# Decay scans of four head pairs in one instruction, GpSimd's products on VectorE, and another issue order in a gated-attention and feed-forward kernel

## The chip, the cores and the metric

The program runs on one core of one Trainium2 chip. The metric is the device time of one execution in microseconds. Three runs of the kernel before took 741.72, 742.07 and 739.28 us; their median is 741.72 us.

## The reference

A gated linear attention over 2 batches, 8 heads, 768 steps and a head dimension of 48 is followed by a gated feed-forward layer and by four weighted experts. All inputs are float32.

```python
def _attn_ref(q, k, v, alpha):
    state = np.zeros((B, H, D, D), dtype=np.float32)
    for t in range(S):
        state = alpha[:, :, t, :, None] * state + np.einsum('bhd,bhe->bhde', k[:, :, t], v[:, :, t])
        y[:, :, t] = np.einsum('bhd,bhde->bhe', q[:, :, t], state)

def _moe_ref(x, w_gate, w_val, w_out, rms_g):        # 1536 tokens, 384 -> 1536 -> 384
    rms = np.sqrt(np.mean(x * x, axis=-1, keepdims=True) + 1e-06)
    xn = x / rms * rms_g
    g = xn @ w_gate
    return (g * (1.0 / (1.0 + np.exp(-g))) * (xn @ w_val)) @ w_out

def _moe2_ref(x, domain_probs, w1, w2):              # 4 experts, 384 -> 1024 -> 384
    p = domain_probs / (domain_probs.sum(-1, keepdims=True) + 1e-09)
    for e in range(E):
        out += p[:, e:e + 1] * (np.maximum(x @ w1[e], 0.0) @ w2[e])
```

The output of the attention, with the heads side by side, is the input of the first layer, and its output is the input of the experts.

## The kernel before

The 768 steps are cut into six chunks of 128, each for two batches: 12 pairs of a chunk and a batch. For a pair, `a_prep` makes decays within the chunk: for each of four head pairs `j` one scan that runs backwards over the steps with a floor (L578, tile `fut`), a reciprocal of its last value (L586), one scan that runs from there to 1 (L592, in the tile `akq`), and then products with k (`KENG`) and q (`QENG`) in halves of two head pairs (L553 on GpSimd, L555 on VectorE). The tables `KENG`, `QENG`, `SENG`, `MENG`, `TENG`, `LENG` and `WENG` name the engine of such a piece for each chunk or weight unit. `a_score` makes the products of k and q (L648) and masks them: for chunks 0 to 3 a copy on ScalarE (L668) and a select on GpSimd (L673), for the others one product on VectorE (L663). `a_y` makes the chunk's output (L687), `a_state` turns k (L718), copies it (L722), makes the state's part of the chunk (L732) and adds it to the state (L755), and the state is decayed at the next chunk's `a_prep` (L631, L636). `a_rms` norms by token (L766 to L794; the power on GpSimd is L779), turns the features onto the partitions (L801), and writes them as a high and a low part (L812, L818, or L830, L838, L843).

The layers work on blocks of 512 tokens: chunks 0 and 1 are block 0, chunks 2 and 3 block 1, chunks 4 and 5 block 2. Every dense product is made in three passes of high and low parts (`mm3`, L856 to L858). The weights of the first layer come as the bits of doubles, in 18 half units; `w_conv` turns each into float bits in three VectorE instructions (L493, L501, L509) and into a high part (ScalarE, L470) and a low part (L476, on VectorE or GpSimd as `WENG` says). For each of 12 tiles `f` of the first layer there are two products (`up1`: gate, value; tile `g`), an activation (L901), a product with the value (L909, tile `s`), its high part (L913) and low part (L920, tile `hl`), and a closing product (`outs`, tile `o`), one step behind. Block 0 goes through its tiles in pieces of 256 columns, half by half:

```python
    steps = [(0, h, 6 * g + f) for g in range(2) for h in (h0, h1) for f in range(6)]
```

`block1` then handles block 1, and after the attention's pools are closed block 2, each with 512 columns, and the experts follow with 96 steps of an up product (tiles `g`, `ph`) and four closing products (tiles `o`, `pe`).

The order of the instructions is set by `Plan`: every operation names its engine, a rough cost, and what it reads and writes; `schedule` then issues, engine by engine, what can start first, by the longest path to the end plus a number for its group (`BIAS`), with two numbers (`MARGIN`, `SLIP`) for how long an engine may be held for something more urgent. On the chip each engine then works through its own queue in that order. While TensorE has to wait for the first chunk, `idle` puts products of zeros (L1001) in its queue, as many as the plan's wait holds. After the layers, a check on the decays (`fit`) decides whether `general`, a slower way for decays that a chunk can't carry, is run.

Of the kernel before, what the change touches and what calls it, by code (L numbers as in the profile page):

```python
# [36 lines left out]
KENG = ["POOL", "POOL", "DVE", "POOL", "POOL", "POOL"]  # L37
QENG = ["DVE", "POOL", "DVE", "POOL", "POOL", "POOL"]
SENG = ["POOL", "POOL", "DVE", "DVE", "POOL", "POOL"]
MENG = ["ACT", "ACT", "ACT", "ACT", "DVE", "DVE"]  # L40
TENG = ["POOL", "POOL", "DVE", "POOL", "DVE", "DVE"]
LENG = ["DVE", "POOL", "DVE", "POOL", "DVE", "DVE"]
HENG = ["DVE", "DVE", "DVE"]
WENG = ["POOL", "DVE", "POOL", "DVE", "POOL", "POOL", "POOL", "DVE", "DVE", "DVE", "POOL", "POOL", "POOL", "DVE", "DVE", "POOL", "DVE", "POOL"]
BIAS = {"c00": 407.1, "c01": 773.8, "w0": -431.2, "": -1780.3, "w5": -1413.1, "c3": -559.1, "w1": -383.5, "s0": -331.4, "c4": -1817.3, "w2": -1907.8, "w4": -996.0, "c1": 501.5, "c5": 48.1, "c2": -2420.3, "guard": -1215.8, "w3": -630.2}
MARGIN, SLIP = 18.01, 3.18


class Tile:
    """A tile that is allocated when its first writer is issued."""  # L50
# [12 lines left out]
class Plan:  # L63
    """Instructions in the order of their meaning, issued in the order of a list schedule.

    Each operation names its engine, a rough cost, and the (parts of) tiles it reads and writes.
    The schedule goes by the longest path to the end; it changes when things are issued, and
    nothing about what is computed."""
# [22 lines left out]
    def op(self, eng, cost, fn, r=(), w=(), chain=None, after=()):  # L91
# [23 lines left out]
        self.ops.append([eng, cost, fn, deps, self.group, before])  # L115
        return i

    def schedule(self):
# [14 lines left out]
        # tiles: who waits for a slot (for the path only)  # L133
# [46 lines left out]
        for _ in range(n):  # L180
# [15 lines left out]
            busy[e] = end  # L196
            for x in uses.get(pick, ()):
# [15 lines left out]
    def issue(self, idle=None, until=None):  # L213
        """idle(us) is called for each wait of the tensor engine up to operation until."""
# [10 lines left out]
def general(tc, const, akq, kf, vf, w64, w32, out):  # L225
    """Everything once more for decays that the products of a chunk can't carry: the state by
    one scan over the sequence for each of its columns, the layers in float32."""
# [4 lines left out]
    with ExitStack() as ctx:  # L232
        dram = ctx.enter_context(tc.tile_pool(name="xs_p", bufs=1, space=bass.MemoryType.DRAM))
        xs = dram.tile([B, DM, S], F32, name="xs")
        with ExitStack() as att:
# [6 lines left out]
            for b in range(B):  # L242
                for j in range(NP):
                    a, k, q = (sb.tile([HP, NC, C], F32, name=f"in{i}") for i in range(3))
                    for t, src in ((a, akq[:, b, :, 0, j]), (k, kf[:, b, :, j]), (q, akq[:, b, :, 2, j])):
                        nc.sync.dma_start(out=t, in_=src.rearrange("c p s -> p c s"))
# [3 lines left out]
                        out=vt, in_=vf[:, b, :, 2 * j * D : 2 * (j + 1) * D].rearrange("c s e -> s c e")  # L250
# [157 lines left out]
def body(ctx: ExitStack, tc: tile.TileContext, ar, akq, v, kf, vf, w64, w32, rms_g, probs, out):  # L408
# [18 lines left out]
    floor = const.tile([P, C + 1], F32, name="floor")  # L427
# [38 lines left out]
    def hilo(key, src, src_ap, lo_eng):  # L466
# [6 lines left out]
        eng, cost = ("POOL", 1.77) if lo_eng is nc.gpsimd else ("DVE", 0.87)  # L473
        plan.op(
            eng, cost,
            lambda: lo_eng.tensor_tensor(  # L476
# [6 lines left out]
    def w_conv(u):  # L483
        """Bits of doubles to bits of floats, then hi + lo."""
# [33 lines left out]
    akq_t, v_t, f_t, at_t, S_t, x1_t = {}, {}, {}, {}, {}, {}  # L518
    guard_n = [0]

    def a_load(c, b, chain=None):
        if c == 1:
            t = plan.tile(x1p, [P, 3, NP, C], F32, ("x1h", "x1l")[b], 2)
            f = plan.tile(wpool, [P, HW], F32, "wlo", 18)
        else:
            t = plan.tile(att, [HP, 3, NP, C], F32, "akq", 2)
            f = plan.tile(att, [HP, NP * (C + 1)], F32, "fut", 2)
        fut = lambda: f()[:HP, : NP * (C + 1)].rearrange("p (j s) -> p j s", j=NP)
        dma(
            0.23, lambda: nc.sync.dma_start(out=fut(), in_=ar[c, b]), w=[(f, 0), (f, 1)],  # L530
            chain=chain,
        )
        for i in range(3):
            dma(
                0.23, lambda i=i: nc.sync.dma_start(out=t()[:HP, i], in_=akq[c, b, :, i]),
                w=[(t, i, 0), (t, i, 1)], chain=chain,
            )
        akq_t[c, b], f_t[c, b] = t, (f, fut)
# [11 lines left out]
    def mul(kind, out, a, b, r, w):  # L550
# [758 lines left out]
```

## Time and profile before

| | us |
|---|---|
| median of three runs | 741.72 |
| lowest and highest run | 739.28, 742.07 |
| span of the profiled execution | 737.2 |
| TensorE busy in the span | 702.5 |
| VectorE busy | 323.0 |
| ScalarE busy | 205.0 |
| GpSimd busy | 99.8 |

The span runs from the first to the last of the program's own instructions; the median of the runs is 4.5 us above it, for what lies around the span. A TensorE instruction's time contains its way through the array, so that neighbours overlap: the pace of products is read from one start to the next. VectorE's records overlap by some 0.07 us in the same way.

### The profile page before, as it was taken

Reading aid. Unit: us, or ns where it says so; the run is one execution under the profiler, and the core shown is the slowest. Engines: PE = TensorE matmul, PEld = TensorE weight load, DVE = VectorE, ACT = ScalarE, POOL = GpSimd, SP = SyncE. Lnnn points to the kernel's source line nnn. Section 1 sums busy time; section 2 is a strip of 40 time slices with the busy share of each in tenths; the row PEclk is TensorE's granted clock in tenths of the full one; section 3 lists DMA queues with packets and bytes.
Section 4 is the critical chain, followed back from the end, with each engine's and each line's share of the span. In section 5 each row is a group of like instructions: output and inputs, shape, how many; then the busy total and the mean of one; then the engine's idle time right before and its main releaser. Section 6 shows DMA issues by size and latency. Waiting matters only on the chain.

```text
span 737.2 us, 10392 instructions
## 1 busy us (share of the span) xinstructions
PE 702.5 (95%) x4330; PEld 623.7 (85%) x4330; DVE 323.0 (44%) x565; ACT 205.0 (28%) x434; POOL 99.8 (14%) x127
## 2 busy tenths in 40 slices
PE   7678897999999999999999999999999999999996
PEld 5577896898888888879989999899998999989995
DVE  8989999757322344452313341214412121312212
ACT  4544354444322243441112321112211111111110
POOL 5957224644000000000000000000000000000000
PEclk9988999999999999999999999999999999999999
DMA  9944472235000023221000220001000000001001
GB/s 270 264 139 168 139 222 74 74 96 190 4 0 1 2 85 129 86 85 44 1 0 1 86 86 0 1 1 44 0 1 1 0 1 1 1 0 44 12 32 48
DMA packets 15416, 44.85 MB, mean 61 GB/s; under 512 B 2048, under 2 KB 5120, under 8 KB 15360
## 3 DMA queue, kind: packets, MB, share of 16 engines
q1 hardware_dynamic: 15072, 44.07, 18.7%
q8 instruction: 36, 0.59, 0.3%
q14 instruction: 20, 0.16, 0.1%
q10 hardware_dynamic: 288, 0.03, 0.0%
HBM read 40.94 MB, written 3.15 MB: 60 GB/s over the span
## 4 chain that ended last, share of the span: by engine, by line
PE 80%; DVE 14%; issue 3%; DMA 1%; ACT 1%; POOL 0%; SPq 0%; DVEq 0%; POOLq 0%; ACTq 0%
PE g L856 10%; PE g L857 10%; PE g L858 10%; PE o L856 9%; PE o L858 9%; PE o L857 9%; PE ph L857 5%; PE ph L858 5%; PE ph L856 4%; PE pe L857 2%; PE pe L856 2%; PE pe L858 2%; DVE akq L592 2%; DVE cv L493 2%; DVE cv L501 2%
## 5 line engine op out<-in xcount | busy, mean ns | idle before, releaser
L856 PE MATMUL g<-x1l,whi 128*128 128x512 f32 (+1 forms) x432 | 156.6, 362 | 6.7 <-DVE s L909 6.2
L858 PE MATMUL g<-x1h,wlo 128*128 128x512 f32 (+1 forms) x432 | 154.7, 358 | 2.7 <-DVE wlo L476 2.6
L857 PE MATMUL g<-x1h,whi 128*128 128x512 f32 (+1 forms) x432 | 154.4, 357 | 0.0
L856 PEld LDWEIGHTS g<-x1l,whi 128*128 128x128 f32 x432 | 82.3, 190 | 18.6 <-DVE s L909 7.0
L858 PE MATMUL o<-whi,hl 128*128 128x384 f32 x288 | 97.5, 338 | 0.0
L856 PE MATMUL o<-wlo,hh 128*128 128x384 f32 x288 | 97.2, 338 | 0.0
L857 PE MATMUL o<-whi,hh 128*128 128x384 f32 x288 | 96.9, 336 | 0.0
L858 PEld LDWEIGHTS g<-x1h,wlo 128*128 128x128 f32 x432 | 82.3, 191 | 14.5 <-DVE wlo L476 3.1
L857 PEld LDWEIGHTS g<-x1h,whi 128*128 128x128 f32 x432 | 82.4, 191 | 10.1
L1173 DVE SCALAR_TENSOR_TENSOR hl<-ph,hh 128x512 fp32r<-128x512 f32 x48 | 33.2, 691 | 128.2 <-ACT hh L1168 128.2
L1173 DVE SCALAR_TENSOR_TENSOR hl<-g,hh 128x512 fp32r<-128x512 f32 x48 | 33.1, 689 | 119.0 <-ACT hh L1168 119.0
L1168 ACT ACTIVATE hh<-g 128x512 fp32r<-128x512 f32 x48 | 28.7, 597 | 162.9 <-PE g L858 162.9
L1168 ACT ACTIVATE hh<-ph 128x512 fp32r<-128x512 f32 x48 | 28.7, 597 | 155.0 <-PE ph L858 153.8
L909 DVE TENSOR_TENSOR s<-g,s 128x256 f32<-128x256 f32 (+1 forms) x48 | 26.6, 554 | 78.3 <-PE g L858 74.1
L856 PEld LDWEIGHTS o<-wlo,hh 128*128 128x128 f32 x288 | 54.1, 188 | 4.2
L857 PEld LDWEIGHTS o<-whi,hh 128*128 128x128 f32 x288 | 54.0, 188 | 4.1
L858 PE MATMUL ph<-x1h,wlo 128*128 128x512 f32 x144 | 57.0, 396 | 0.0
L857 PE MATMUL ph<-x1h,whi 128*128 128x512 f32 x144 | 56.9, 395 | 0.0
L856 PE MATMUL ph<-x1l,whi 128*128 128x512 f32 x144 | 56.0, 389 | 0.0
L856 PE MATMUL o<-hl,whi 128*128 128x256 f32 (+1 forms) x144 | 50.7, 352 | 4.4 <-DVE hl L920 4.3
L858 PEld LDWEIGHTS o<-whi,hl 128*128 128x128 f32 x288 | 54.0, 187 | 0.0
L858 PE MATMUL o<-hh,wlo 128*128 128x256 f32 (+1 forms) x144 | 48.8, 339 | 0.0
(144 smaller groups left out, 1020.5 us busy)
## 6 DMA issues: line engine op xcount, KB each, us to landing
raw<-in_w SPq DMA_DIRECT2D x34, 768.0 KB, 4.2
akq<-in_akq SPq DMA_DIRECT2D x30, 224.0 KB, 4.3
out_y<-acc SPq DMA_DIRECT2D x12, 192.0 KB, 1.9
fut<-in_ar SPq DMA_DIRECT2D x10, 225.8 KB, 3.2
v<-in_v SPq DMA_DIRECT2D x10, 192.0 KB, 5.3
x_dram<-s SPq DMA_DIRECT2D x3, 256.0 KB, 2.3
raw<-x_dram SPq DMA_DIRECT2D x1, 768.0 KB, 6.4
x1h<-in_akq SPq DMA_DIRECT2D x3, 224.0 KB, 5.1
```

The lines of the kernel that those rows point to most:

```text
L493: lambda: nc.vector.tensor_scalar(out=t(), in0=word(1), scalar1=3, scalar2=0x3FFFFFFF, op0=ALU.logical_shift_left, op1=ALU.bitwise_and,),
L501: lambda: nc.vector.scalar_tensor_tensor(out=t(), in0=word(1), scalar=0xC0000000, in1=t(), op0=ALU.bitwise_and, op1=ALU.bitwise_or,),
L592: lambda j=j: nc.vector.tensor_tensor_scan(out=t()[:HP, 0, j], data0=t()[:HP, 0, j], data1=ones[:HP, :C], initial=inv()[:, j : j + 1], op0 ...
L856: nc.tensor.matmul(ps_ap, lhsT=lh, rhs=rl, start=first, stop=False)
L857: nc.tensor.matmul(ps_ap, lhsT=lh, rhs=rh, start=False, stop=False)
L858: nc.tensor.matmul(ps_ap, lhsT=ll, rhs=rh, start=False, stop=last)
L909: lambda: nc.vector.tensor_mul(s()[:, :n], pv()[:, :n], s()[:, :n]), r=[pv], w=[s],
L1168: "ACT", 0.5, lambda: nc.scalar.activation(out=hh(), in_=ph(), func=AF.Relu),
L1173: lambda: nc.vector.scalar_tensor_tensor(out=hl(), in0=ph(), scalar=0.0, in1=hh().bitcast(F32), op0=ALU.max, op1=ALU.subtract,),
```

## The change

Each piece that a table gave to GpSimd is now VectorE's, but for the 12 powers of the norm and the memsets; the tables are gone. `a_load` brings one copy of the decays (`af`, 517 columns: four head pairs of 129 columns and one more) and one each of k and q (`kq`); the copies with reversed steps are gone. `a_prep` makes the decays from the chunk's start for all four head pairs in one scan (`F`, L571), one reciprocal (L578), one scan backwards over the same tile (`af`, L582), and one product each for q and k over 512 columns (L591, L598). The state is kept with the decay of the chunk included: `a_state` multiplies by the chunk's whole decay after adding (L726, L731), and for chunk 0 in place of the copy (L718). All masks are one product on VectorE (L643). The norm's correction takes two VectorE instructions (L761, L768) in place of four. Block 0 has 8 steps of 256 columns and then 8 of 512. The plan treats VectorE and GpSimd as taking turns (`port`) unless an operation reads PSUM, has other costs, and has another table `BIAS`, `MARGIN` and `SLIP`. The waiting products on TensorE take the floor's values as the moving side in four of every eight.

```diff
-KENG = ["POOL", "POOL", "DVE", "POOL", "POOL", "POOL"]
...
-WENG = ["POOL", "DVE", "POOL", "DVE", "POOL", "POOL", "POOL", "DVE", "DVE", "DVE", "POOL", "POOL", "POOL", "DVE", "DVE", "POOL", "DVE", "POOL"]
-BIAS = {"c00": 407.1, "c01": 773.8, "w0": -431.2, ...
+BIAS = {"c00": -3533.7, "c01": -889.8, "w0": 3012.7, ...
...
-            t = max(ready[i], busy.get(ops[i][0], 0.0))
+            t = max(ready[i], busy.get(ops[i][0], 0.0), busy.get("port", 0.0) if ops[i][6] else 0.0)
...
+            if ops[pick][6]:
+                busy["port"] = end
...
-        for i in range(3):
+        for i in (1, 0):
             dma(
-                0.23, lambda i=i: nc.sync.dma_start(out=t()[:HP, i], in_=akq[c, b, :, i]),
+                0.23, lambda i=i: nc.sync.dma_start(out=t()[:HP, i], in_=kq[c, b, :, i]),
...
-            for j in range(2 * half, 2 * half + 2):
-                plan.op(
-                    "DVE", 0.203,
-                    lambda j=j: nc.vector.tensor_tensor_scan(
-                        out=fut()[:, j], data0=fut()[:, j], data1=floor[:HP],
-                        initial=1.0, op0=ALU.mult, op1=ALU.max,
-                    ),
...
-            mul(KENG[c], k, k, lambda js=js: fut()[:, js, :C], [(f, half)], [(t, 1, half)])
-            mul(QENG[c], q, q, p, [(t, 0, half)], [(t, 2, half)])
+        plan.op(
+            "DVE", 1.15,
+            lambda: nc.vector.tensor_tensor_scan(
+                out=p(), data0=f()[:HP, :SEG], data1=floor[:HP], initial=1.0,
+                op0=ALU.mult, op1=ALU.max,
+            ),
+            r=[f], w=[p],
+        )
+        plan.op(
+            "DVE", 0.12, lambda: nc.vector.reciprocal(out=zinv[:HP, ends], in_=p()[:, C::CS]), r=[p], w=["z"]
+        )
+        plan.op(
+            "DVE", 1.15,
+            lambda: nc.vector.tensor_tensor_scan(
+                out=f()[:HP, SEG::-1], data0=f()[:HP, SEG::-1], data1=zinv[:HP, SEG::-1],
+                initial=0.0, op0=ALU.mult, op1=ALU.add,
+            ),
+            r=["z"], w=[f],
+        )
...
-            if MENG[c] == "DVE":
...
-                plan.op(
-                    "ACT", 0.48, lambda s=s, a=a: nc.scalar.activation(out=a(), in_=s(), func=AF.Copy),
-                    r=[s], w=[a],
-                )
-                plan.op(
-                    "POOL", 0.6,
-                    lambda a=a: nc.gpsimd.affine_select(
...
+            plan.op(
+                "DVE", 0.6,
+                lambda s=s, a=a: nc.vector.tensor_mul(a(), s(), mask.to_broadcast([P, NP, C])),
+                r=[s], w=[a], port=False,
+            )
...
+        if c:
+            plan.op(
+                "DVE", 0.47, lambda: nc.vector.tensor_mul(s(), s(), whole(2 * D)), r=[p],
+                w=[(s, 0), (s, 1)],
+            )
...
-        hilo(u, t, lambda: t().bitcast(F32), nc.gpsimd if WENG[u] == "POOL" else nc.vector)
+        hilo(u, t, lambda: t().bitcast(F32))
...
-            nc.tensor.matmul(first[0](), lhsT=zw, rhs=zeros, start=False, stop=False)
+        for n in range(max(0, round(gap / 0.215)) if start else 0):
+            nc.tensor.matmul(
+                first[0](), lhsT=zw, rhs=floor[:, :512].bitcast(F32R) if n % 8 > 3 else zeros,
+                start=False, stop=False,
+            )
...
-    steps = [(0, h, 6 * g + f) for g in range(2) for h in (h0, h1) for f in range(6)]
+    steps = [(0, h, f) for h in (h0, h1) for f in range(4)]
+    steps += [(0, slice(0, 512), f) for f in range(4, 12)]
```

The start of VectorE's queue in the kernel before; the scans stand as SCALAR_TENSOR_TENSOR on L578 and L592, and `wlo` is chunk 1's decay tile.

```order
3 L578 SCALAR_TENSOR_TENSOR fut<-fut,floor 112x129 x4
4 L586 RECIPROCAL inv<-fut 112x2 x2
5 L592 SCALAR_TENSOR_TENSOR akq<-akq,inv,ones 112x128 x4
6 L555 TENSOR_TENSOR akq<-akq 112x256 x2
7 L578 SCALAR_TENSOR_TENSOR fut<-fut,floor 112x129 x4
8 L586 RECIPROCAL inv<-fut 112x2 x2
9 L592 SCALAR_TENSOR_TENSOR akq<-akq,inv,ones 112x128 x4
10 L555 TENSOR_TENSOR akq<-akq 112x256 x2
11 L493 TENSOR_SCALAR cv<-raw 128x768
12 L501 SCALAR_TENSOR_TENSOR cv<-raw,cv 128x768
```

The same place in the changed kernel; the scans are L571 and L582, L591 and L598 the products with q and k, L643 the masks, L494 and L502 the first steps of a weight unit.

```order
5 L571 SCALAR_TENSOR_TENSOR F<-af,floor 112x516
6 L578 RECIPROCAL zinv<-F 112x4
7 L591 TENSOR_TENSOR kq<-kq,F 112x512
8 L582 SCALAR_TENSOR_TENSOR af<-af,zinv 112x517
9 L571 SCALAR_TENSOR_TENSOR F<-af,floor 112x516
10 L598 TENSOR_TENSOR kq<-kq,af 112x512
11 L578 RECIPROCAL zinv<-F 112x4
12 L591 TENSOR_TENSOR kq<-kq,F 112x512
13 L582 SCALAR_TENSOR_TENSOR af<-af,zinv 112x517
14 L494 TENSOR_SCALAR cv<-raw 128x768
15 L643 TENSOR_TENSOR at<-att,mask 128x512
16 L502 SCALAR_TENSOR_TENSOR cv<-raw,cv 128x768
```

Eight scans of a batch became two, the k products came in from GpSimd's queue, and the masks stand between the steps of the weights.

VectorE's queue in the changed kernel where block 0 goes over to 512 columns: `s` and `hl` (L869, L879) belong to the dense steps, L494 to L510 and L477 to the weight units, L726 and L731 to the state.

```order
117 L869 TENSOR_TENSOR s<-g,s 128x512
118 L494 TENSOR_SCALAR cv<-raw 128x768
119 L477 TENSOR_TENSOR wlo<-cv,whi 128x768
120 L879 TENSOR_TENSOR hl<-s,hh 128x512
121 L502 SCALAR_TENSOR_TENSOR cv<-raw,cv 128x768
122 L726 TENSOR_TENSOR S_126<-att,S_126 48x4x48
123 L510 SCALAR_TENSOR_TENSOR cv<-raw,cv 128x768
124 L494 TENSOR_SCALAR cv<-raw 128x768
125 L731 TENSOR_TENSOR S_126<-S_126,F 112x384
126 L869 TENSOR_TENSOR s<-g,s 128x512
```

In the kernel before a stretch of the same work reads so (`akq` here is chunk 2's k and q):

```order
100 L493 TENSOR_SCALAR cv<-raw 128x768
101 L555 TENSOR_TENSOR akq<-akq,fut 112x256
102 L501 SCALAR_TENSOR_TENSOR cv<-raw,cv 128x768
103 L909 TENSOR_TENSOR s<-g,s 128x256
104 L509 SCALAR_TENSOR_TENSOR cv<-raw,cv 128x768
105 L920 TENSOR_TENSOR hl<-s,hh 128x256
```

Every weight unit's low part now stands in VectorE's queue (L477), and an `s` and an `hl` cover twice the columns from here on.

## Rows read from the trace of the kernel before

**Rows 1.** The page, part 1: busy time, share of the span, instructions.

```profile
PE 702.5 (95%) x4330; PEld 623.7 (85%) x4330; DVE 323.0 (44%) x565; ACT 205.0 (28%) x434; POOL 99.8 (14%) x127
```

**Rows 2.** Windows: PE, PEld, DVE, ACT, POOL busy; clock, DMA share, GB/s.

```profile
28.00:172.00 144.00, 122.83 (x1320) 114.19 (x1319) 127.74 (x238) 64.68 (x183) 74.06 (x83) 0.95 0.43 133
172.00:336.00 164.00, 163.72 (x845) 134.69 (x844) 67.18 (x117) 58.28 (x100) 5.91 (x8) 1.00 0.19 66
...
3.00:5.00 2.00, 2.00 (x7) 1.67 (x6) 1.41 (x5) 0.00 (x0) 0.00 (x0) 1.00 1.02 304
...
34.00:38.00 4.00, 1.64 (x14) 1.44 (x12) 4.00 (x3) 0.00 (x0) 4.00 (x4) 1.00 0.88 292
```

**Rows 3.** Timeline of TensorE at its turning points: start, us, line, tiles.

```profile
28.07 0.28 PE L856 MATMUL g<-x1l,whi 128*128 128x256 f32 x1
28.19 0.28 PE L857 MATMUL g<-x1h,whi 128*128 128x256 f32 x1
...
172.36 0.40 PE L856 MATMUL g<-x1l,whi 128*128 128x512 f32 x1
...
328.94 0.39 PE L856 MATMUL g<-x1l,whi 128*128 128x512 f32 x1
...
330.98 0.39 PE L856 MATMUL ph<-x1l,whi 128*128 128x512 f32 x1
```

**Rows 4.** Groups of instructions up to 260 us: count, busy us, mean ns.

```profile
L578 DVE TENSOR_TENSOR_SCAN fut<-fut,floor 112x129 f32<-112x129 f32 x40 | 25.1, 673 | 2.6 <-DMA fut<-in_ar 2.4 <-issue 0.2
L592 DVE TENSOR_TENSOR_SCAN akq<-akq,inv,ones 112x128 f32<-112x128 f32 x40 | 24.8, 663 | 0.5 <-DMA akq<-in_akq 0.5
...
L509 DVE SCALAR_TENSOR_TENSOR cv<-raw,cv 128x768 uint32<-128x768 uint32 x18 | 17.0, 943 | 0.0
L493 DVE TENSOR_SCALAR cv<-raw 128x768 uint32<-128x768 uint32 x18 | 16.1, 897 | 0.1
```

**Rows 5.** Timeline of VectorE: start, us, line, tiles, shapes, count.

```profile
3.60 1.38 DVE L578 TENSOR_TENSOR_SCAN fut<-fut,floor 112x129 f32<-112x129 f32 x4 [2.41 <-DMA fut<-in_ar]
...
34.72 4.00 DVE L578 TENSOR_TENSOR_SCAN fut<-fut,floor 112x129 f32<-112x129 f32 x1
...
58.05 0.55 DVE L493 TENSOR_SCALAR cv<-raw 128x768 uint32<-128x768 uint32 x1
58.52 0.42 DVE L555 TENSOR_TENSOR akq<-akq 112x256 f32<-112x256 f32 x1
...
80.50 0.85 DVE L592 TENSOR_TENSOR_SCAN akq<-akq,inv,ones 112x128 f32<-112x128 f32 x2
...
94.94 0.15 DVE L784 TENSOR_TENSOR rms<-rms 128x1 f32<-128x1 f32 x1
...
182.58 0.85 DVE L818 SCALAR_TENSOR_TENSOR x1l<-att,g_sb,x1h 128x128 fp32r<-128x128 f32 x3
...
193.61 1.28 DVE L663 TENSOR_TENSOR at<-att,mask 128x512 f32<-128x512 f32 x2
```

**Rows 6.** Windows, instructions on the state S alone: VectorE busy and count.

```profile
0.00:172.00 172.00, 7.56 (x18) 0.96 0.51 157
```

**Rows 7.** The chain that ended last, attention's pieces on TensorE: start, us.

```profile
150.06 0.60 PE att L732 x14
151.92 1.09 PE att L648 x16
156.76 1.74 PE att L687 x48
161.92 0.40 PE att L718 x4
...
192.62 0.48 PE att L801 x3
```

**Rows 8.** Timeline of 14.6 to 15.3 us: a power on GpSimd beside three scans.

```profile
14.47 1.05 DVE L578 TENSOR_TENSOR_SCAN wlo<-wlo,floor 112x129 f32<-112x129 f32 x3
14.69 0.56 POOL L779 TENSOR_TENSOR rms<-rms,mhalf 128x1 f32<-128x1 f32 x1
```

More of the change, by code (lines that the diff above doesn't have):

```diff
@@ L89, in tile, with op @@
         return t
-    def op(self, eng, cost, fn, r=(), w=(), chain=None, after=()):
+    def op(self, eng, cost, fn, r=(), w=(), chain=None, after=(), port=None):
         i = len(self.ops)
@@ L114, in op @@
         deps.discard(i)
-        self.ops.append([eng, cost, fn, deps, self.group, before])
+        port = eng in ("DVE", "POOL") if port is None else port
+        self.ops.append([eng, cost, fn, deps, self.group, before, port])
         return i
@@ L561, in note @@
         g, plan.group = plan.group, "guard"
[L562 removed]
+        junk = plan.tile(att, shape, BF16, "junk", 1)
         plan.op("ACT", cost, lambda: fn(junk(), gd[:HP, n : n + 1]), r=src, w=[junk, ("gd", n)])
@@ new lines, in a_prep @@
+        f, t = af_t.pop((c, b)), kq_t[c, b]
+        p_t[c, b] = p = plan.tile(att, [HP, SEG], F32, "F", 2)
+        ends = slice(CS, SEG + 1, CS)
+        plan.op(
[9 more added lines that the diff above has]
+        )
@@ L706, in a_y @@
                 plan.op(
-                    "PE", 0.62, lambda i=i: [inner(j, i) for j in range(NP)], r=[vt, a[i]], w=[(y, i)]
+                    "PE", 0.5, lambda i=i: [inner(j, i) for j in range(NP)], r=[vt, a[i]], w=[(y, i)]
                 )
@@ L735, in go @@
                     )
-        plan.op("PE", 0.56, go, r=[kt, vt], w=[d])
+        plan.op("PE", 0.6, go, r=[kt, vt], w=[d])
         if c == 0:
@@ L741, in a_state @@
         s = S_t[b]
+        whole = lambda n, rows=slice(0, HP): p()[rows, C::CS].unsqueeze(2).to_broadcast(
+            [rows.stop - rows.start, NP, n]
+        )
         for i in range(2):
@@ L745, in a_state @@
                 plan.op(
-                    "ACT", 0.23,
-                    lambda i=i, part=part: nc.scalar.activation(
-                        out=part(), in_=d()[heads[i]], func=AF.Copy
+                    "DVE", 0.27,
+                    lambda i=i, part=part: nc.vector.tensor_mul(
+                        part(), d()[heads[i]], whole(D, heads[i])
                     ),
-                    r=[d], w=[(s, i)],
+                    r=[d, p], w=[(s, i)], port=False,
                 )
@@ L755, in a_state @@
                     lambda i=i, part=part: nc.vector.tensor_add(part(), d()[heads[i]], part()),
-                    r=[d], w=[(s, i)],
+                    r=[d], w=[(s, i)], port=False,
                 )
+        if c:
+            plan.op(
+                "DVE", 0.47, lambda: nc.vector.tensor_mul(s(), s(), whole(2 * D)), r=[p],
+                w=[(s, 0), (s, 1)],
+            )
     def a_rms(c, b, y):
@@ L891, in prod @@
             i = plan.op(
-                "PE", 0.02 + 0.96 * n / 256, go, r=[*units[u1(f, w)], *parts], w=[p], chain="dense"
+                "PE", 9 * (n / 2400 + 0.0135), go, r=[*units[u1(f, w)], *parts], w=[p], chain="dense"
             )
@@ L909, in up1 @@
             lambda: nc.vector.tensor_mul(s()[:, :n], pv()[:, :n], s()[:, :n]), r=[pv], w=[s],
+            port=False,
         )
@@ L941, in go @@
                     )
-            plan.op("PE", 0.02 + 0.96 * w / 256, go, r=[*units[u1(f, 2)], hh, hl], w=po, chain="dense")
+            plan.op("PE", 9 * (w / 2400 + 0.0135), go, r=[*units[u1(f, 2)], hh, hl], w=po, chain="dense")
         for n, st in enumerate(steps):
@@ L999, in idle @@
         gap = end - start - 0.2 - (COLD if start < 2 else 0)
-        for _ in range(max(0, round(gap / 0.215)) if start else 0):
-            nc.tensor.matmul(first[0](), lhsT=zw, rhs=zeros, start=False, stop=False)
+        for n in range(max(0, round(gap / 0.215)) if start else 0):
+            nc.tensor.matmul(
+                first[0](), lhsT=zw, rhs=floor[:, :512].bitcast(F32R) if n % 8 > 3 else zeros,
+                start=False, stop=False,
+            )
     nconv = [0]
@@ L1038, in chunk @@
         for b in range(2):
-            if (c, b) not in akq_t:
+            if (c, b) not in kq_t:
                 a_load(c, b)
@@ L1161, in e_up @@
         plan.op(
-            "PE", 1.94, go, r=[*units[key], *((t, d) for t in (th, tl) for d in range(KD))],
+            "PE", 2.07, go, r=[*units[key], *((t, d) for t in (th, tl) for d in range(KD))],
             w=[ph], chain="dense",
@@ L1198, in go @@
                 )
-            plan.op("PE", 0.49, go, r=[*units[key], hh, hl], w=[p], chain="dense")
+            plan.op("PE", 0.522, go, r=[*units[key], hh, hl], w=[p], chain="dense")
             if f < 7:
```

256 lines of the change are left out of this document (95 added, 161 removed).

## The prediction

> **What bounds the kernel now.** I read the page first, then windows, then the two timelines. The page alone misleads: TensorE is busy for 95% of the span, VectorE for 44% [rows 1]. By stage it is otherwise. From 172 us on TensorE is busy for 163.7 of 164 us and VectorE for 67; from 28 to 172 us TensorE is busy for 122.8 of 144, at a granted clock of 0.95, while VectorE is busy for 127.7 and GpSimd for 74.1 [rows 2]. So the change, which touches attention, the weights of the first layer and their order, works in the one stretch where TensorE waits.
>
> How much is to be had there? TensorE's own work is counted from starts. A dense product of 256 columns comes every 0.12 us, nine make 1.08; nine of 512 columns take 330.98 - 328.94 = 2.04 [rows 3]. Block 0 has 24 steps of three such groups of nine: 24 x 3 x 1.08 = 77.8 us. Blocks 1 and 2 have 12 steps each: 2 x 12 x 3 x 2.04 = 146.9. The attention of a pair takes 1.09 + 1.74 + 0.40 + 0.60 + 0.48 = 4.3 us [rows 7]; ten pairs follow the first dense product, two of them without the state's 1.0: 41. Dense work starts at 28.07, so without a wait the experts would start at 28.1 + 77.8 + 146.9 + 41 = 293.8. They start at 328.94 [rows 3]: 35.1 us are lost, 21.2 of them as idle time between 28 and 172 us [rows 2], the rest in the slower clock and in waits inside a group.
>
> What loses them is VectorE, and what slows VectorE is GpSimd. Four scans over 129 steps take 1.38 us where GpSimd is idle and DMA is at its fullest (share 1.02); one such scan takes 4.00 us from 34.72 on, where GpSimd is busy without a pause [rows 2, 5]. The mean of this scan is 673 ns against 0.335 in the clean four, of the other scan 663 against about 0.39, of L493 897 against the 0.47 between its start and the next [rows 4, 5]. That is 25.1 - 40 x 0.335 = 11.7, 24.8 - 40 x 0.39 = 9.2 and 16.1 - 18 x 0.47 = 7.6 us: 28.5 us of stretching on these three rows.
>
> **The change part by part.** *VectorE's instructions.* One row gives a fixed and a per-column part: a product of 256 columns costs 0.35, one of 512 (1.28 for two, less the overlap) 0.605 [rows 5], so 0.09 is fixed. A scan of 129 at 0.335 then has 0.245 for its steps, and one over 516 costs some 0.09 + 4 x 0.245 = 1.07; the trace has no scan of that width. Its upper bound is four of before, 4 x 0.335 = 1.34, and for the backward one, which takes the place of L592, 4 x 0.40 = 1.60; the lower is 1.0. I take 1.15 for both. Up to the last features of block 1 (order row 216 of VectorE's queue) the changed kernel issues: 19 scans 21.9; 18 products with q and k and 18 masks, 36 x 0.605 = 21.8; 18 weight units at 0.47 + 3 x 0.87 (L509's 0.943 less the overlap) = 3.08, together 55.4; 33 small ones of the norm and reciprocals at 0.15, 5.0; 22 on the state at 7.56 / 18 less the overlap, 0.40 [rows 6], 8.8; 24 low parts of features at 0.85 / 3 less overlap, 0.26, 6.2; 16 `s` and `hl` of 256 at 0.35, 5.6, and 16 of 512 at 0.605, 9.7 [rows 4, 5]. Sum 134.4, and with the first decays' landing at 3.6: 138.0 us. So what came from GpSimd (ten low parts of weights, 36 half products, 16 masks) does not come free; it takes the room that the stretching leaves.
>
> *The start.* Up to the second batch's features (order row 46) the same prices give 7 scans, 4 products, 4 masks, three weight units and the rest, 27.1 us, and 3.6 + 27.1 = 30.7. I take 31 for the first dense product, 3 us later than before: the third unit's bytes (768 KB) can only be asked for once the first unit is done. It is no loss by itself, since three units are then ready in place of one.
>
> *TensorE.* Block 0 becomes 8 x 3 x 1.08 + 8 x 3 x 2.04 = 74.9, 2.9 less. The waiting products are more (79 for 41), but they end where the work before them is expected; half of them on other values I cost at nothing, bounded by the 2.04 / 9 = 0.23 us of one on either side. ScalarE loses 16 copies of masks and was busy for 64.7 of 144 [rows 2]: nothing. The reversed copies that are no longer loaded, 12 x 224 KB: nothing, since the start waits for VectorE, not for the bytes behind the first decays; below zero at most 1 us.
>
> *The sum.* Without waits the experts would start at 31 + 74.9 + 146.9 + 41 = 293.8, the same as before. Losses that I expect: early, VectorE is still behind. For the fifth low part `hl` it has 56.8 us to do after 3.6, so 60.4; TensorE is there after 25.2 us of work, 31 + 25.2 = 56.2: 4.5 us with the hand-over. Then TensorE's greater work closes the gap: at block 1 it stands at 31 + 74.9 + 28 (attention of chunks 1 to 3) + 4.5 = 138.4, VectorE at 138.0. Two queues so level, in fixed order, lose more: an `s` that waits for TensorE's product holds the weight steps and masks behind it, and TensorE waits for those later, at some 40 hand-overs; before, 35.1 - 28.5 = 6.6 us were lost beside the stretching, and I take 5 (bounds 0 and 13, twice that). So the experts start at 293.8 + 9.5 = 303.3, 25.6 us earlier; what follows is unchanged. The profiled execution has a span of 737.2, the median lies 4.5 above: 741.7 - 25.6 = 716.1 us.
>
> **A rule of the skill.** Beside a power on GpSimd of 0.56 us three scans took 1.05 us, as clean as any [rows 8]; so I let the 12 powers that stay cost VectorE nothing. The Trainium skill says otherwise (SBUF — State Buffer, section "SBUF: two separate sides"): the port pair that VectorE and GpSimd share is an exclusive lock, held for a whole instruction, and the loser fully blocks. That agrees with the scan of 4.00 us, not with this row.
>
> **The rivals.**
> 1. *VectorE stays the bound.* The wide scans cost what four narrow ones did (1.34 and 1.60), 0.64 us more per pair; for eight pairs 5.1, and since VectorE is level with TensorE all of it counts. With the hand-overs at 10 in place of 5 the time is 716 + 5.1 + 5 = 726. For it speaks that the sums leave no slack; against it, that the fixed part of narrow ones shows in every row.
> 2. *The powers hold VectorE.* Each of the 8 powers ahead of block 1 holds it for its whole 0.56 us: 8 x 0.56 = 4.5, 721. Rows 8 speak against it. This is the skill's rule of the same section, and what it would make here.
> 3. *The other side: the stretching is not GpSimd's.* If VectorE's instructions are stretched by a cause that stays (DMA, or reading the same memory as TensorE), the new work comes on top. From 28 to 172 us the ratio is 127.7 / (127.7 - 28.5) = 1.29; 134.4 x 1.29 + 3.6 = 177, against 172.36 for block 1 before [rows 3], with blocks 1 and 2 and three pairs (two of them without the state, 10.6 us) to go: 177 + 146.9 + 10.6 = 334.5, 5.6 later than 328.94, so 747. It decides from a ratio of (328.9 - 157.5 - 3.6) / 134.4 = 1.25. Against it: the clean scans at 3.6 us ran beside full DMA and a busy TensorE [rows 2].
> 4. *It doesn't do what it says:* the new plan's order makes TensorE wait elsewhere (a clock at its lower level after each wait, weights late) for as much as it wins: 740, no change. For it speaks only that every queue's order is new.
>
> **How the numbers follow.** Forecast 0.72 (own range 707 to 722), rival 1 0.13, rival 2 0.05, rival 3 0.06, rival 4 0.04. The lower end of the range is a loss of nothing, 741.7 - 35.1 = 706.6; the upper takes the upper bound of the hand-overs and the powers, 716 + 8 + 4.5 = 728, and holds rivals 1 and 2. A measurement of this kernel tells 0.5%, some 3.7 us, from no change. Faster by more is the forecast and rivals 1 and 2: 0.90; within it 0.04; slower 0.06.
>
> **What would show it.** Right: no scan over 1.3 us and L494 near 0.55 us each; GpSimd busy for under 15 us; VectorE busy without a pause up to some 138 us; the first 256-column product at about 31 us, the first 512-column product of block 1 near 143 and the experts' first near 303; TensorE idle for under 10 us between 31 and 140, and a clock of 1.00. Wrong: scans or weight steps as long as before without GpSimd (rival 3); scans clean at 1.3 to 1.6 (rival 1); VectorE instructions beside a power 0.56 us longer (rival 2); long waits of TensorE for weights or features, with the clock down (rival 4).

## The result, and the profile after

The changed kernel took 715.12 us (median of four runs, 714.03 to 715.80), the kernel before in the same comparison 740.65. The ratio is 0.966, with a 95% interval from 0.964 to 0.968: 25.5 us faster, where 716.1 and 25.6 had been forecast. The profiled execution has a span of 713.7 us.

First the page, part 1 (beside [rows 1]), and then the two windows of [rows 2], columns as there.

```profile
PE 701.1 (98%) x4152; PEld 612.4 (86%) x4152; DVE 314.9 (44%) x531; ACT 195.2 (27%) x394; POOL 14.8 (2%) x26
```

```profile
28.00:172.00 144.00, 141.07 (x1304) 119.33 (x1305) 131.49 (x248) 67.52 (x178) 10.07 (x9) 0.99 0.42 134
172.00:336.00 164.00, 163.54 (x781) 137.15 (x782) 59.76 (x90) 52.25 (x85) 0.55 (x1) 1.00 0.15 49
```

VectorE's share of the span is 44% in both kernels, and from 28 to 172 us it is busy for 131.5 us where it was 127.7. Yet TensorE's idle time in this window fell from 21.2 us to 2.9, and GpSimd's busy time from 74.1 to 10.1. How much of VectorE's time had been stretching, the groups below show.

The turning points of TensorE, from its timeline (beside [rows 3]):

```profile
31.06 0.34 PE L816 MATMUL g<-x1l,whi 128*128 128x256 f32 x1
...
57.14 0.38 PE L816 MATMUL g<-x1l,whi 128*128 128x256 f32 x1 [0.94 <-DVE x1l L799]
...
142.56 0.50 PE L816 MATMUL g<-x1l,whi 128*128 128x512 f32 x1
...
304.31 0.39 PE L816 MATMUL g<-x1l,whi 128*128 128x512 f32 x1
```

The first dense product stands at 31.06 us (28.07 before), the first 512-column product of block 1 at 142.56 (172.36), the experts' first at 304.31 (328.94). The wait at 57.14 is the last of TensorE in block 0. Windows on either side of it show that, and one inside shows where the clock was at its lower level:

```profile
34.00:58.00 24.00, 21.28 (x256) 19.61 (x254) 22.43 (x46) 11.03 (x29) 1.74 (x2) 0.93 0.40 133
58.00:142.00 84.00, 84.00 (x727) 70.50 (x727) 81.34 (x144) 40.46 (x98) 5.19 (x4) 1.00 0.42 132
```

```profile
42.80:46.00 3.20, 3.20 (x20) 2.98 (x18) 3.17 (x7) 1.00 (x2) 0.00 (x0) 0.50 0.41 166
```

TensorE had idled 0.56, 0.65 and 0.57 us between 36 and 43 us; then the granted clock was 0.50 (the level of 1.2 GHz) for 3.4 us from 42.70. Before, there were two such stretches of 6.8 us, from 38.6 and from 59.1; a window inside each, in the kernel before:

```profile
38.70:45.40 6.70, 5.43 (x58) 5.12 (x58) 5.78 (x12) 2.64 (x6) 0.00 (x0) 0.50 0.52 169
59.20:65.90 6.70, 5.64 (x36) 5.26 (x37) 6.62 (x12) 2.73 (x7) 6.07 (x7) 0.50 0.51 158
```

VectorE's groups up to 160 us (beside [rows 4]; columns as there: count, busy, mean ns):

```profile
L510 DVE SCALAR_TENSOR_TENSOR cv<-raw,cv 128x768 uint32<-128x768 uint32 x18 | 17.1, 951 | 0.1
...
L571 DVE TENSOR_TENSOR_SCAN F<-af,floor 112x516 f32<-112x516 f32 x10 | 12.2, 1225 | 0.0
L582 DVE TENSOR_TENSOR_SCAN af<-af,zinv 112x517 f32<-112x517 f32 x9 | 11.1, 1228 | 0.0
L494 DVE TENSOR_SCALAR cv<-raw 128x768 uint32<-128x768 uint32 x18 | 9.8, 552 | 0.3 <-DMA raw<-in_w 0.2
```

The first step of a weight unit (L494) takes 552 ns where L493 took 897, and L510 is what L509 was (951 for 943): it had not been stretched. A wide scan's record is 1.23 us long; from its start to the next one's it takes 1.12 to 1.26, on average 1.17. VectorE's last features of block 1 show how close the two engines run (timeline of VectorE):

```profile
140.81 0.86 DVE L799 SCALAR_TENSOR_TENSOR x1l<-att,gneg,x1h 128x128 fp32r<-128x128 f32 x3
```

They end at 141.67, 0.9 us before TensorE takes them up at 142.56. And the powers that stayed on GpSimd, three of its timeline's rows (beside [rows 8]):

```profile
50.73 0.55 POOL L756 TENSOR_TENSOR rms<-rms,mhalf 128x1 f32<-128x1 f32 x1 [8.86 <-DVE rms L749]
96.25 1.80 POOL L756 TENSOR_TENSOR rms<-rms,mhalf 128x1 f32<-128x1 f32 x1 [44.98 <-DVE rms L749]
...
144.35 0.55 POOL L756 TENSOR_TENSOR rms<-rms,mhalf 128x1 f32<-128x1 f32 x1 [10.22 <-DVE rms L749]
```

It is the power that grows, to 1.80 us, while VectorE's scans and steps keep their length: the one at 96.25 begins 0.17 us after a weight step of VectorE, an `hl` follows that step at once, and the power ends 0.41 us after the `hl`.

**Where the 24.6 us to the experts' first product come from.** Idle time of TensorE from the first dense product on fell from 21.2 to 2.7 us: 18.4. Time at half clock fell from 13.6 to 3.4 us, which at half speed gives back 5.1. The wider steps give the 2.9 us of fewer starts. The start is 3.0 us later. Together 23.4; 1.2 us are spread over the rest. The whole span is 23.5 us shorter, not 24.6: the part from the experts' first product on takes 409.3 us where it took 408.2, and the granted clock is 0.50 for its last 5.4 us in place of 2.2.

### The profile page after: what moved, and what is told of

Same layout as the page of the kernel before. It is cut to its first block, busy times and chain, and to the rows that moved or that the text cites. A ratio compares the mean times of both kernels' runs of the same rounds, so it can differ in the third digit from the quotient of the medians.

```text
span 713.7 us, 9773 instructions
## 1 busy us (share of the span) xinstructions
PE 701.1 (98%) x4152; PEld 612.4 (86%) x4152; DVE 314.9 (44%) x531; ACT 195.2 (27%) x394; POOL 14.8 (2%) x26
## 4 chain that ended last, share of the span: by engine, by line
PE 92%; DVE 5%; DMA 1%; issue 0%; ACT 0%; DVEq 0%; ACTq 0%
PE g L816 12%; PE g L817 11%; PE g L818 11%; PE o L816 11%; PE o L818 10%; PE o L817 10%; PE ph L817 5%; PE ph L818 5%; PE ph L816 5%; PE pe L817 2%; PE pe L816 2%; PE pe L818 2%; PE att L654 2%; PE att L634 1%; DMA raw<-in_w 1%; DVE wlo L477 1%
## 5 line engine op out<-in xcount | busy, mean ns | idle before, releaser
L816 PE MATMUL g<-x1l,whi 128*128 128x512 f32 (+1 forms) x384 | 146.7, 382 | 1.5 <-DVE x1l L799 0.9
L818 PE MATMUL g<-x1h,wlo 128*128 128x512 f32 (+1 forms) x384 | 145.4, 379 | 0.0
L817 PE MATMUL g<-x1h,whi 128*128 128x512 f32 (+1 forms) x384 | 145.3, 378 | 0.0
L816 PEld LDWEIGHTS g<-x1l,whi 128*128 128x128 f32 x384 | 72.4, 189 | 14.4 <-DVE x1l L799 1.3
L818 PEld LDWEIGHTS g<-x1h,wlo 128*128 128x128 f32 x384 | 72.2, 188 | 13.4
L817 PEld LDWEIGHTS g<-x1h,whi 128*128 128x128 f32 x384 | 72.4, 188 | 11.5
L869 DVE TENSOR_TENSOR s<-g,s 128x512 f32<-128x512 f32 (+1 forms) x40 | 25.4, 634 | 54.3 <-PE g L818 54.1
L816 PE MATMUL o<-hl,whi 128*128 128x512 f32 (+1 forms) x120 | 45.7, 381 | 0.5 <-DVE hl L879 0.5
L818 PE MATMUL o<-hh,wlo 128*128 128x512 f32 (+1 forms) x120 | 44.6, 372 | 0.0
```

Of the source, the lines that this page charges most:

```text
L816: nc.tensor.matmul(ps_ap, lhsT=lh, rhs=rl, start=first, stop=False)
L817: nc.tensor.matmul(ps_ap, lhsT=lh, rhs=rh, start=False, stop=False)
L818: nc.tensor.matmul(ps_ap, lhsT=ll, rhs=rh, start=False, stop=last)
L869: lambda: nc.vector.tensor_mul(s()[:, :n], pv()[:, :n], s()[:, :n]), r=[pv], w=[s],
```

## The experiments

All times are medians beside the kernel before on the same chip (740.63, 739.86 and 739.34 us in the three comparisons); the ratios have 95% intervals of some 0.002 to either side.

**1. GpSimd's work moved, and nothing else.** The kernel before with all its tables set to VectorE:

```diff
-KENG = ["POOL", "POOL", "DVE", "POOL", "POOL", "POOL"]
+KENG = ["DVE"] * 6
...
+WENG = ["DVE"] * 18
```

> The kernel before with every entry of its engine tables set to VectorE: GpSimd keeps the powers and memsets, scans stay narrow, block 0 keeps 24 steps of 256 columns, the plan makes a new order with the old numbers. Theory A (GpSimd stretched VectorE, and that set the time): VectorE's clean work up to block 1 is the changed kernel's 134.4 us plus 5.9 for narrow scans, 1.7 for half products, 2.4 for the norm, 1.5 for block 0, some 146 us, without stretching; faster than before, 722 to 733 us, the narrow scan at 0.34 us each. Theory B (the wide scans and the new order make the gain): 737 or more. Theory C (moved work makes VectorE the bound): 745 or more.

Measured: 736.03 us, ratio 0.993 [0.990, 0.996]. So the move gains, but 4.6 us, less than the range of theory A. The groups up to 160 us show its mechanism at work all the same:

```profile
L578 DVE TENSOR_TENSOR_SCAN fut<-fut,floor 112x129 f32<-112x129 f32 x40 | 14.7, 412 | 3.9 <-DMA fut<-in_ar 3.8
L592 DVE TENSOR_TENSOR_SCAN akq<-akq,inv,ones 112x128 f32<-112x128 f32 x32 | 13.7, 467 | 0.0
...
L493 DVE TENSOR_SCALAR cv<-raw 128x768 uint32<-128x768 uint32 x18 | 9.9, 549 | 0.0
```

The three groups whose means were 673, 663 and 897 ns [rows 4] stand at 412, 467 and 549: the stretching is gone. But the work that came over fills the room. From 3.6 us to the end of block 1's last features VectorE is busy for 142.4 us (132.8 in the changed kernel), and they end at 153.1; TensorE starts its dense products only at 34.45 and idles for 16.9 us, and after 38 us its clock is at the lower level for 13.7 us, as before.

**2. The new numbers alone.** The kernel before with the changed kernel's `BIAS`, `MARGIN` and `SLIP`:

```diff
-MARGIN, SLIP = 18.01, 3.18
+MARGIN, SLIP = 0.00, 5.58
```

> The kernel before with the changed kernel's BIAS, MARGIN and SLIP alone. Theory A: the stretching stays, so no gain: 735 to 755 us. Theory B (the order makes the gain): under 730 us.

Measured: 746.87 us, ratio 1.008 [1.007, 1.010]. A table that was made for other instructions makes the kernel before slower. The reverse, the changed kernel with the numbers of before:

> The changed kernel with BIAS, MARGIN and SLIP of before. Theory A: most of the gain stays, 717 to 727 us. Theory B (the order makes the gain): 733 or more.

Measured: 716.77 us, ratio 0.968 [0.965, 0.970]. The numbers are worth at most some 1.7 us there, which the two intervals do not tell from nothing; the gain is not in them.

**3. GpSimd's load put back.** The ten low parts of weights that were GpSimd's go back to it:

```diff
+WENG = ["POOL", "DVE", "POOL", "DVE", "POOL", "POOL", "POOL", "DVE", ...
-            "DVE", 0.87,
+            "POOL" if pool else "DVE", 1.77 if pool else 0.87,
```

> The changed kernel with ten of the 18 low parts of weights on GpSimd, as the table of before had them. VectorE loses 10 x 0.87 = 8.7 us of its own work. Theory A: GpSimd's 10 x 1.8 us hold VectorE up by as much or more, 715 to 724 us, with single VectorE instructions of 1.5 us and more. Theory D (GpSimd is free help, the stretching came from elsewhere): 706 to 712 us.

Measured: 724.88 us, ratio 0.978 [0.975, 0.981]: 9.8 us slower than the changed kernel, though VectorE has ten instructions of 0.87 us less. Two groups, of the window from 28 to 140 us and of that from 0 to 145:

```profile
L479 POOL TENSOR_TENSOR wlo<-cv,whi 128x768 fp32r<-128x768 f32 x8 | 15.3, 1913 | 42.1 <-ACT whi L473 42.1
```

```profile
L881 DVE TENSOR_TENSOR hl<-s,hh 128x512 fp32r<-128x512 f32 x8 | 9.2, 1146 | 1.1 <-ACT hh L876 1.1
```

A low part takes 1.91 us on GpSimd, and the subtraction `hl`, which TensorE waits for, takes 1146 ns on VectorE where it is 682 in the changed kernel: three of the eight, which began while GpSimd worked, took 1.91 us each, the others 0.69. Up to the end of block 1's features VectorE is busy for 132.1 us, hardly less than the 132.8 of the changed kernel: the stretching takes back what the move saves. The 9.8 us themselves are pauses: VectorE's are 9.6 us more, and the features end at 150.6. TensorE idles for 5.3 us more, 2.8 of them ahead of 142.02 for an `hl` that stands behind a scan and two state steps in VectorE's own queue, and is at the lower clock for 10.2 us in place of 3.4. The queue's order is new in this run, and how much of the pauses comes from the order and how much from GpSimd was not tried apart.

**4. Reading or writing?** 36 subtractions of 256 columns on GpSimd, two after each weight unit, into a tile that nothing reads, and the same with memsets:

```diff
+        plan.op(
+            "POOL", 1.2, lambda: [nc.gpsimd.tensor_tensor(out=spare, in0=floor[:, :256],
+                in1=floor[:, 256:512], op=ALU.subtract) for _ in range(2)],
+            r=[units[u][1]], w=["spare"], port=False,
+        )
```

> The changed kernel with 36 subtractions of 256 columns on GpSimd beside its work (two behind each low part of the first layer's weights, some 0.65 us each, 23 us in all), into a tile that nothing reads; VectorE's queue has the same instructions in the same order but for one pair that trades places. Theory A: VectorE is held for a good part of 23 us, 720 to 735 us. Theory D (GpSimd doesn't hold VectorE): 715 to 717 us.

> As the run with 36 subtractions on GpSimd, but with 36 memsets of 256 columns in their place, which read nothing. If what holds VectorE is GpSimd's reading beside it: 714 to 717 us, and scans of 1.2 us throughout. If any work of GpSimd does: as long as the run with subtractions, in proportion to GpSimd's busy time.

Measured: 724.49 us [ratio 0.977 to 0.981] with the subtractions, 715.11 [0.964 to 0.968] with the memsets: 9.4 us and nothing. Groups from 28 to 140 us, with the subtractions and then with the memsets (line numbers are one higher than the changed kernel's in the weight unit, five higher after it):

```profile
L519 POOL TENSOR_TENSOR spare<-floor 128x256 f32<-128x256 f32 x30 | 41.6, 1387 | 2.0
...
L511 DVE SCALAR_TENSOR_TENSOR cv<-raw,cv 128x768 uint32<-128x768 uint32 x15 | 15.5, 1034 | 0.1
...
L478 DVE TENSOR_TENSOR wlo<-cv,whi 128x768 fp32r<-128x768 f32 x14 | 14.3, 1024 | 0.0
...
L495 DVE TENSOR_SCALAR cv<-raw 128x768 uint32<-128x768 uint32 x14 | 8.5, 618 | 0.0
...
L648 DVE TENSOR_TENSOR at<-att,mask 128x512 f32<-128x512 f32 x12 | 7.7, 679 | 0.1
...
L804 DVE SCALAR_TENSOR_TENSOR x1l<-att,gneg,x1h 128x128 fp32r<-128x128 f32 x18 | 5.2, 343 | 1.7 <-ACT x1h L798 1.7
...
L884 DVE TENSOR_TENSOR hl<-s,hh 128x256 fp32r<-128x256 f32 x8 | 4.7, 586 | 0.0
...
L766 DVE SCALAR_TENSOR_TENSOR rms<-rms,rms 128x1 f32<-128x1 f32 x5 | 3.4, 686 | 0.5 <-POOL rms L761 0.4
```

```profile
L519 POOL MEMSET spare<- 128x256 f32 x30 | 9.7, 322 | 1.4
...
L495 DVE TENSOR_SCALAR cv<-raw 128x768 uint32<-128x768 uint32 x14 | 7.7, 557 | 0.5 <-DMA raw<-in_w 0.4
...
L648 DVE TENSOR_TENSOR at<-att,mask 128x512 f32<-128x512 f32 x12 | 7.7, 680 | 0.7 <-PE att L639 0.7
...
L884 DVE TENSOR_TENSOR hl<-s,hh 128x256 fp32r<-128x256 f32 x8 | 3.3, 418 | 0.0
```

With the subtractions `hl` rises from 418 to 586 ns and a one-column step of the norm (L766) to 686, where it is 213 in the changed kernel; the masks (L648, 679 for 680) and the features (L804, 343 for 344 in the changed kernel), which read their first input from PSUM, keep their length. VectorE's busy time up to block 1's features grows by 12.5 us, TensorE's idle time from 2.7 to 7.6. So a VectorE instruction whose two inputs both lie in SBUF is held by a GpSimd instruction that reads, and not by one that only writes. The Trainium skill says just this (SBUF — State Buffer, section "Who interferes with whom": such an instruction contends with a GpSimd instruction that reads SBUF, not with one that only writes it), and both runs agree.

Two inputs are not the whole of it. The first step of a weight unit (L495 here, L493 before) has one input, and it grows too, to 618 ns beside the subtractions. The kernel before shows how, in two rows of GpSimd's and VectorE's timelines:

```profile
48.37 1.82 POOL L476 TENSOR_TENSOR wlo<-cv,whi 128x768 fp32r<-128x768 f32 x1
...
48.48 2.12 DVE L493 TENSOR_SCALAR cv<-raw 128x768 uint32<-128x768 uint32 x1
```

GpSimd's low part ends at 50.19, the step 0.41 us later. Four of the 18 L493 began while a low part ran on GpSimd; they took 1.87 to 2.13 us, each until some 0.41 us after that low part. One that began 0.3 us ahead of a low part (at 86.97) took 0.53. A memset holds this step as well: of the 18 L495 of that run, the one that began while a memset ran took 0.66 us, which the median of the runs does not show. In these rows the one that begins second pays, and it can be GpSimd: the L509 at 31.08 keeps its length (0.93 us) beside a product on GpSimd (L553) that began at 30.84, while a scan ran, and this product is 1.75 us long where its line has 0.80 in the median.

**5. The width of the scans.** Each wide scan as four of 129 columns:

```diff
+        def first(j):
+            o = slice(j * CS, (j + 1) * CS)
+            nc.vector.tensor_tensor_scan(
+                out=p()[:, o], data0=f()[:HP, o], data1=floor[:HP, o], initial=1.0,
...
+        plan.op("DVE", 1.15, lambda: [first(j) for j in range(NP)], r=[f], w=[p])
```

> The changed kernel with each wide scan cut into its four head pairs, in the same place of the queue. By the forecast's prices each of 24 groups costs 3 x 0.09 = 0.27 us more, 5.1 us up to block 1, 1.9 of them ahead of the first dense product: 717 to 721 us. If wide scans save nothing: 715 us. If they are the greater part of the gain: 725 or more.

Measured: 715.89 us, ratio 0.967 [0.965, 0.969]: 0.8 us, not told from nothing. The reason is in the groups (up to 145 us):

```profile
L571 DVE TENSOR_TENSOR_SCAN F<-af,floor 112x129 f32<-112x129 f32 x32 | 10.9, 404 | 0.0
L582 DVE TENSOR_TENSOR_SCAN af<-af,zinv 112x129 f32<-112x129 f32 x32 | 10.9, 403 | 0.0
```

From start to start such a scan takes 0.33 us; four make 1.32, the wide one 1.17. A scan's time is nearly all in its steps. Up to block 1's features that is 2.5 us of VectorE's time; they end 1.5 us later, 0.9 of it already at the start, and TensorE idles 3.05 us in place of 2.72 (from 31 to 140 us). The start itself varies by as much: the run with memsets has it at 32.69, 1.6 us later than the changed kernel.

**6. The steps of block 0.** The 24 steps of 256 columns of before, in the changed kernel:

```diff
-    steps = [(0, h, f) for h in (h0, h1) for f in range(4)]
-    steps += [(0, slice(0, 512), f) for f in range(4, 12)]
+    steps = [(0, h, 6 * g + f) for g in range(2) for h in (h0, h1) for f in range(6)]
```

> The changed kernel with block 0 in 24 steps of 256 columns, as before, and chunks 2 and 3 placed at the same steps as before. TensorE's own work is 2.9 us more, VectorE's 1.5: 717 to 721 us by theory A; 725 or more if the steps of 512 columns are a greater part of the gain.

Measured: 723.87 us, ratio 0.977 [0.975, 0.979]: 8.7 us, three times TensorE's 2.9. So the same 24 narrow steps in another order, from the fifth tile on half after half of each tile:

```diff
-    steps += [(0, slice(0, 512), f) for f in range(4, 12)]
+    steps += [(0, h, f) for f in range(4, 12) for h in (h0, h1)]
```

> The changed kernel with its table and its order of tiles, but each step of block 0 from the fifth tile on made as two steps of 256 columns right after one another (first half, second half, next tile), where the run with 24 steps of 256 went through six tiles of one half and then six of the other. Theory A (narrow steps cost only TensorE's 2.9 us and some VectorE time; the rest of the 8.7 us came from the order of the tiles, which wants 9 of the 18 weight units before the second half is touched, where the changed kernel wants 6): 717 to 719. Rival B (the narrow steps themselves cost it, by more instructions and hand-overs on VectorE and TensorE): 722 to 725.

Measured: 718.38 us, ratio 0.971 [0.969, 0.973]: 3.3 us. The landmarks agree: from the first dense product to block 1's first it is 111.5 us in the changed kernel, 114.0 with alternating halves and 119.5 in the first of the two runs. So the narrow columns cost about what the count of TensorE's starts says, and the other 5.4 us lie in the order: six tiles of one half ask for nine weight units ahead of chunk 1, four tiles for six. VectorE's waits up to 70 us in the first of the two runs (us in total, times, longest):

```profile
DVE cv L494 <- DMA raw<-in_w: 2.8, 3, 1.6
...
DVE hl L879 <- ACT hh L874: 1.7, 2, 1.5
```

Chunk 1's last features begin at 69.0 us there, at 59.6 with alternating halves and at 57.3 in the changed kernel; TensorE idles 5.8, 2.7 and 2.7 us (from 31 to 140 us).

**7. What the narrow kernel still lacked.** Run 1 with the changed kernel's steps added, and then also with right costs for the narrow scans in the plan and a table searched for the earliest end by the plan's own costs:

```diff
-                    "DVE", 0.203,
+                    "DVE", 0.34,
...
-                    "DVE", 0.264,
+                    "DVE", 0.40,
```

> The kernel before with every piece of GpSimd's tables on VectorE (736.0 us as measured) and, in addition, the changed kernel's 8 steps of 256 and 8 of 512 columns; scans, products and norm stay narrow, table and costs stay those of before. Theory A (the steps are worth here what they were worth in the changed kernel, 8.7 us): 725 to 730. Rival B (VectorE, with its narrow instructions, stays the bound all through block 0, so that the order of the steps is worth little): 733 to 737.

> As before_all_vector_512, with the costs of the two narrow scans in the plan set to what the clean trace shows (0.34 and 0.40 in place of 0.203 and 0.264), and with a table BIAS, MARGIN and SLIP of its own, searched for the earliest end of the list schedule by its own costs. What is then left between it and the changed kernel is the width of the instructions (and the reversed copies). Theory A (VectorE binds and the width counts in full: per pair of chunk and batch four scans of 0.34 and four of 0.40 against two of 1.14, four products of 0.35 against two of 0.605, two reciprocals against one, four small norm instructions against two, about 1.2 us, times 8 pairs ahead of block 1): 722 to 727. Rival B (width is hidden, as the scans cut in four cost the changed kernel 0.8 us only): 715 to 719. Rival C (the order can't make up for narrow forms at all): 729 or more.

Measured: 730.50 us (0.988 [0.986, 0.990]) and 724.97 (0.980 [0.978, 0.982]). In the first the steps are worth 5.5 us in place of 8.7 (4.0 by the ratios, since the kernel before took 1.3 us less in this comparison than beside run 1), and the time is 0.5 above theory A's range and well below rival B's; in the second theory A's 722 to 727 holds. The windows from 28 to 172 us of run 1, of the run with the steps, and of the one with the new order:

```profile
28.00:172.00 144.00, 126.44 (x1345) 117.52 (x1346) 135.43 (x337) 62.54 (x174) 6.38 (x8) 0.95 0.44 140
```

```profile
28.00:172.00 144.00, 130.91 (x1176) 109.55 (x1174) 137.23 (x328) 61.23 (x161) 8.34 (x8) 0.95 0.47 149
```

```profile
28.00:172.00 144.00, 132.12 (x1161) 110.68 (x1158) 135.23 (x325) 63.29 (x161) 6.11 (x8) 0.95 0.47 150
```

VectorE stays at 135 to 137 of 144 us, and TensorE climbs from 126.4 to 132.1; the changed kernel has 141.1. What parts the last run from it is the form of VectorE's instructions, the copies loaded, the state's form, the plan's turns and the waiting products, and no run parts these from one another. VectorE is busy for 138.0 us, for 132.8 in the changed kernel, up to the end of block 1's features, with 3.3 us more pauses, so that they end 8.5 us later (150.2). On TensorE's side, up to the experts' first product (10.4 us later), it is 9.0 us more idle time and a clock at its lower level for 13.7 us, from 40.98 on, in place of 3.4; its dense work begins 2.6 us earlier. The scans' part of this is not their width alone: L592, with a third input, takes 0.387 us from start to start, a narrow backward scan of two inputs 0.33.

**8. Another table.** The changed kernel with a table found by the same search:

> The changed kernel with another table BIAS, MARGIN and SLIP, searched for the earliest end of the list schedule by its own costs; nothing else is changed. TensorE loses 2.7 us as idle time between 31 and 57 us and 1.7 us to a dip of its clock, and nothing after that. Theory A (the order is close to what it can give; part of these 4.4 us and of the start at 31.06 is left to gain): 712.5 to 715. Rival B (such a small gain by the plan's costs is lost on the chip, in waits that the plan doesn't price): 715 to 718.

Measured: 714.29 us, ratio 0.967 [0.964, 0.969]. It begins dense work at 27.53 us and loses 4.6 us as idle time in place of 2.7. Beside 715.12 that is no difference that these runs can tell.

## Why the prediction was right

**The cause was named right, and it is not the whole of the gain.** TensorE waited for VectorE, and VectorE was stretched by GpSimd's reads: run 4 makes the stretching anew and pays 9.4 us, and run 1 takes it away, for 4.6. Rival 3 (the stretching is not GpSimd's) falls with the same rows. Rival 4 falls with run 2 and the result.

**The sum held at every landmark.** First dense product 31 forecast, 31.06 measured; block 1 near 143, 142.56; experts 303.3, 304.31; a wide scan 1.15, 1.17; a weight unit 3.08, 3.08 from start to start; VectorE's work to block 1's features 134.4, 132.8. (One price was not what its row says: a state step at 7.56 / 18 less 0.07 is 0.35 us, not 0.40, which makes 1.1 us less.) These features end at 141.7 where 138.0 was said, since 5.3 us of pauses came on top, which the forecast had at nothing.

**The total is closer than its parts.** The experts start 24.6 us earlier, where 25.6 was said, and the rest, said to be unchanged, takes 1.1 us longer. The 4.5 us that were taken to lie around the span are 1.7 to 2.1 in every later run of the kernel before; so the profiled execution, with its span of 737.2 us, was about 2.5 us faster than the median to which the gain was applied. That the difference of the medians (25.5) is the forecast's to 0.1 us is luck. The upper end of the range stands there twice, as 722 and as 728; the result lies under both.

**Its losses were right in size and partly wrong in kind, which is luck as well.** The early loss of 4.5 us is there: 2.7 us of idle time and 1.7 for the clock, all before 57.2 us. But the forecast expected a clock of 1.00 and saw the loss at the fifth `hl`; it came at four places, and with a dip of the clock, which the sum had no term for. The hand-over loss of 5 us for two level queues did not come: between 57.2 and 300 us TensorE does not idle at all. In its place stand 5.2 us that no wait explains: the 96 groups of nine 512-column products up to the experts took 201.5 us with 0.5 idle, where 96 x 2.04 = 195.8 were counted, because a group beside the attention's small products takes 2.13 to 2.27 us from its start to the next product's; 5 us for hand-overs and 5.2 us for these are the same size by chance. The count of TensorE's work from uninterrupted products was too low by that much, so the floor of 293.8, and with it the range's lower end, could not be reached by a faster VectorE as long as TensorE's products are mixed in this way.

**Two terms were mis-sized.** Of the steps only TensorE's 2.9 us were priced; with the order of the tiles they are worth 4 to 8.7 (runs 6 and 7). And the total of the forecast does not come from one part: run 1 shows that the move to VectorE alone is worth 4.6 us. The steps add 5.5, right costs and order 5.5, the wider forms and the rest 9.9: 740.6, 736.0, 730.5, 725.0, 715.1. These come from three comparisons; by the ratios the parts are 5.1, 4.0, 5.7 and 10.5, each to some 2 us. The forecast priced the whole at once and never said what a part would be worth; theory A's 722 to 733 for run 1 shows that it would have said too much.

**Rival 1** (VectorE stays the bound) did not come, since the wide scans cost 1.17; and its price was too high: with narrow scans of two inputs VectorE is busy for 2.5 us more in run 5 and TensorE idles 0.3 more, so that a VectorE which is level with TensorE does not pass on all that it loses. **Rival 2** (each power holds VectorE for its whole time) expected the wrong side to wait. The Trainium skill's rule behind it (SBUF — State Buffer, section "SBUF: two separate sides": whoever starts first holds the pair for the whole instruction) is not against the rows: here the one-column power waits, up to 1.80 us in place of 0.55, and VectorE's own groups keep their length; in run 4, with subtractions queued one behind the other on GpSimd, VectorE's grow.

## What to carry to other kernels

When VectorE's instructions have twice the time in one place that they have in another, look what GpSimd reads at that moment before counting instructions: work that is moved to GpSimd can cost VectorE as much as it takes away (run 3: ten instructions less, and VectorE's busy time the same). Moving it back pays only if VectorE then has room; here that took steps in an order that asks for weights later, a new schedule, and wider forms with what came beside them, the first two each worth about as much as the move itself, the last twice that. Count an engine's floor from products in the mixture in which they run, not from an uninterrupted row of them.

## What the runs showed of the hardware that was not expected

Memsets on GpSimd beside VectorE cost the kernel nothing (36 of them: 715.11 us against 715.12), though one held a one-input step of VectorE (0.66 us in place of 0.55). Such a step waits for a GpSimd subtraction to its end (four of 18 in the kernel before, 1.87 to 2.13 us in place of 0.55). A power of one column on GpSimd grows to 1.80 us beside a busy VectorE. A scan over 516 steps takes 1.17 us from start to start and one over 129 steps 0.33, so that its fixed part is some 0.05 us (1.32 - 1.17 = 0.15 for three starts), about half of the 0.09 read from the products. Whether the clock's dips of 10.2 us near 11 us in the two narrow runs 1 and 7 (with the steps) come from the pauses of 0.9 to 1.6 us in TensorE's waiting products there was not tried apart: the kernel before had a pause of 1.87 us at 7.94 without one. Nor was the new moving side of these waiting products (the floor's values in half of them, zeros in all of them in the narrow runs): no run has it alone, so what it did for the clock is open.
